# Transnormer attention and a squared-ReLU MLP on one core: the opening's loads and steps in another order, seven clamps on GpSimd, batch three's last queries loaded elsewhere

## The chip, the core and the metric

One core of a Trainium2 chip runs the whole kernel. The metric is device time in microseconds (us); lower is better. The core has five engines that each work through their own list of instructions in order and wait for each other by semaphores: PE (TensorE, matrix products), DVE (VectorE), ACT (ScalarE), POOL (GpSimd) and SP (SyncE, which issues nearly all transfers here). Sixteen DMA engines move data between HBM and the on-chip memory.

## What is computed

```python
def _attn_ref(q, k, v, g_norm):                    # q, k, v: (8, 8, 576, 64)
    kv = np.einsum('bhsd,bhse->bhde', k, v)
    out = np.einsum('bhsd,bhde->bhse', q, kv)
    rms = np.sqrt(np.mean(out * out, axis=-1, keepdims=True) + 1e-06)
    return (out / rms * g_norm).astype(np.float32)

def _moe_ref(x, w_in, w_out):                      # x: (4608, 512), w_in: (512, 2048), w_out: (2048, 512)
    h = x @ w_in
    r = np.maximum(h, 0.0)
    return ((r * r) @ w_out).astype(np.float32)
```

The attention output, transposed to (batch, token, head, feature), is x. q, k and v are float32; the two weight matrices come as float64 and are turned into float32 on the chip.

## The kernel before

**Strips.** The 4608 tokens are 36 tiles of 128, in nine strips of four tiles. Each strip has a first product (x by w_in, then ReLU and square) and a second one (by w_out). Strip zero multiplies plainly in its first product (`up_first`, L898) and by a seven-product scheme in its second (`down`, L857). Strip one uses the seven-product scheme in its first product (`up`) and a two-level one in its second (`down_deep`, `small_products`, L852), which takes its weights as 14 blocks that SP streams from HBM (`stream`, L955 and L961, tile `w_blk`). From strip two on both products are two-level, and part of the first product's weights are streamed too (L949). The attention of later tokens is spread over the strips as a list of small steps, `slices`, that `attend` works off.

**Transfers.** Nothing is scheduled by a tool: instructions stand on each engine in the order in which the program emits them. SP issues one transfer after another; a transfer that has to wait, for a buffer or for the landing of an earlier one (only a few may be in flight), holds all that stand behind it. Queries of batches two and up are read in pieces of 32 features, four transfers to a head pair (`load`, L124); the last 64 rows of each batch, which do not fill a tile, come apart (`load_rest` for keys and values, L163; `load_q_rest` for queries, L171 for batches zero and one, L177 with eight transfers of 16 KB for the others). From strip one on such loads stand in the queues `drips` and `rest_drips`, from which one is taken every so many steps (`drip`), unless `quiet` is true. `transposed_query` puts the next ones into these queues.

**The opening.** The first strip's tokens are batch zero's first 512 rows. For each head pair p: T(0, p) transposes queries on PE (L407) and copies them on ACT (L409); K(0, p) multiplies keys and values on PE (L435, the last rows from `k_rest` and `v_rest` at the end) and copies on ACT (L440, L441); Q(p) multiplies queries with that (L585), squares on ACT and sums on DVE (L488); N(p) takes the root (ACT) and its inverse and scales (DVE); F(p) transposes the result (L611) and copies it with g_norm to `xT` (L612); U(p, tiles) are the first product's matmuls for that p (`first_up`, L622), which need weight piece p.

**Weight conversion.** Each matrix comes as 16 pieces of 512 KB float64 (`load_piece`, L240, eight buffers `raw`). For a piece ACT makes two passes (`convert_on_act`, L254 and L258; here `size` and `low`), and DVE four steps (`conversion`): a clamp (L266), a shift (L268), a merge (L272) and a sum (L275). The intermediate `w_c` has four buffers. In the opening pieces zero to three are converted by hand-placed steps (`first_piece`), the clamps of one to three on GpSimd; the others go in pairs by `convert` between the steps of strip zero. Pieces four and five have their ACT passes after the opening's list.

Of the kernel before, what the change touches and what calls it, by code (L numbers as in the profile page):

```python
# [15 lines left out]
ALU = mybir.AluOpType  # L16
# [4 lines left out]
def kernel(  # L21
# [34 lines left out]
    nc = tc.nc  # L56
    P = 128
    B, H, S, D = q.shape
# [3 lines left out]
    NP = H // 2  # L62
# [9 lines left out]
    N_STRIP = N_TILE // NT  # L72
    DEEP = 1
    DEEP_UP = 2
    FIRST_SENT = 9
    SQ = 32
    Q_ON_PE = 2
# [78 lines left out]

    squares = lambda t: t.rearrange("p h d -> p (h d)").rearrange("p (k q f) -> p k q f", k=4, f=SQ)

    def load_rest(b, eng):
        h = b % 2  # L160
        half = slice(REST * h, REST * (h + 1))
        for t, src in ((k_rest[half], k), (v_rest[half], v)):
            eng.dma_start(out=t, in_=src[b, :, C * P : S].rearrange("h s d -> s h d"))  # L163

    def load_q_rest(b, eng, one=None):
        h = b % 2
# [81 lines left out]
    def convert_on_act(i, parts=(0, 1)):  # L248
        view = lambda dt: raw[i].bitcast(dt).rearrange("p b (n two) -> p b n two", two=2)
        low, high, high_f = view(U32)[:, :, :, 0], view(I32)[:, :, :, 1], view(FP32)[:, :, :, 1]  # L250
        r = view(I32)[:, :, :, 0]
        if 0 in parts:
            c = wtmp.tile([P, 2, WN // 2], FP32, name="w_c", tag="w_c")
            nc.scalar.activation(c, high_f, AF.Abs)  # L254
            words[i] = c, r, high

        if 1 in parts:
            nc.scalar.activation(r, low, AF.Copy, scale=2.0**-29)  # L258

    def conversion(i, dest, eng=nc.vector):  # L260

        c, r, high = words.pop(i)
        ci = c.bitcast(I32)


        yield eng.tensor_scalar(out=c, in0=c, scalar1=LEAST, scalar2=MOST, op0=ALU.max, op1=ALU.min)  # L266

        yield nc.vector.tensor_scalar(  # L268
            out=ci, in0=ci, scalar1=3, scalar2=0x3FFFFFFF, op0=ALU.logical_shift_left, op1=ALU.bitwise_and
        )  # L270

        yield nc.vector.scalar_tensor_tensor(  # L272
            out=ci, in0=high, scalar=-(2**30), in1=ci, op0=ALU.bitwise_and, op1=ALU.bitwise_or
        )
        yield nc.vector.tensor_tensor(out=dest.bitcast(I32), in0=ci, in1=r, op=ALU.add)  # L275
# [73 lines left out]
    nc.scalar.sqrt(one, one)  # L349

    load_next()
    load_rest(0, nc.sync)
    load_next()
    for p in range(2, NP):
        load(0, p, nc.sync, "q")
        load_piece()
        load(0, p, nc.sync, "kv")
        next(to_load)
    load_more(0)
    g_col = const.tile([P, 1], FP32, name="g_col")  # L360
# [20 lines left out]
    def transposed_query(b, p):  # L381
        while any(f == load and a[:2] == (b, p) for f, a in drips):
            drip()
        t = main.pop(("q", b, p))
        if b >= Q_ON_PE:
            qT[b, p] = qt_pool.tile([P, C, P], FP32, name="qT", tag="qT")
            nc.vector.transpose(out=flat(qT[b, p]), in_=flat(t))
            if b % 2 and p == NP - 1:
                while any(f == load_q_rest and a[0] <= b for f, a in (*rest_drips, *drips)):
                    drip(not drips)  # L390
                nc.vector.transpose(
                    out=open_rest(b).rearrange("p q (k t) -> p q k t", k=4),
                    in_=squares(q_rest[b // 2]).rearrange("p k q f -> p q k f"),
                )
            drip_queries()
            if p == NP - 1 and b + 1 < B:
                (rest_drips, drips)[b % 2 == 0].extend((load_q_rest, (b + 1, nc.sync, a)) for a in range(4))
            return
        ps = apsum.tile([P, C, P], FP32, name="t_ps", tag="at")
        if (b, p) == (0, 0):  # L400
            keep_busy(ps[:, 0], 7)
        for c in range(C):
            if b:
                nc.tensor.transpose(ps[:, c, :], flat(t[:, c]), ident)
                continue
            for h in range(2):
                nc.tensor.matmul(ps[ts(h, D), c, :], lhsT=t[:, h, c], rhs=ident, start=True, stop=True)  # L407
        qT[b, p] = qt_pool.tile([P, C, P], FP32, name="qT", tag="qT")
        nc.scalar.copy(qT[b, p], ps)  # L409
        if (b, p) == (1, NP - 1):  # L410
            drip_queries()
# [186 lines left out]
    def first_piece(i, n):  # L598

        if i not in first_steps:  # L600
            first_steps[i] = conversion(
                i, w_in[:, i % KH, 0, i // KH * 2 : i // KH * 2 + 2], nc.gpsimd if i else nc.vector
            )
        for _ in range(n):
            next(first_steps[i])

# [87 lines left out]
    )  # L694
    U = first_up
    size, low = (lambda i: (act, (i, (0,)))), (lambda i: (act, (i, (1,))))
    slices += [(T, (0, 0)), (K, (0, 0)), (T, (0, 1)), (Q, (0,)), (K, (0, 1)), (N, (0,)), size(0), (piece, (0, 1))]
    slices += [(T, (0, 2)), (Q, (1,)), low(0), (piece, (0, 1)), (K, (0, 2)), (N, (1,)), (F, (0,)), (T, (0, 3))]
    slices += [(piece, (0, 1)), (Q, (2,)), (piece, (0, 1)), size(1), (K, (0, 3)), low(1), (N, (2,)), (F, (1,))]
    slices += [(piece, (1, 4)), (Q, (3,)), size(2), low(2), (U, (0, [0, 1, 2])), size(3), (F, (2,)), (piece, (2, 4))]  # L700
    slices += [(U, (1, [0, 1, 2])), (N, (3,)), low(3), (piece, (3, 4)), (U, (2, [0, 1])), (F, (3,)), (U, (2, [2]))]
    slices += [(U, (3, [0, 1, 2]))]
    ready[0] = len(slices)
    def query_pairs(b):
        first_n = b // 2 * PAIR + (C if b % 2 else 0)
# [636 lines left out]
    attend(ready[0])  # L1342
    opening.close()
    apsum = psums.enter_context(tc.tile_pool(name="apsum", bufs=2, space=bass.MemoryType.PSUM))
    for i in range(NP, NP + 2):
        convert_on_act(i)
    acted[0] = NP + 2
    for s in range(N_STRIP):
        attend(ready[s])
        if s == DEEP_UP - 1:  # L1350
# [23 lines left out]
        for i, (w, fn, a) in enumerate(steps):  # L1374
# [33 lines left out]
            if s:  # L1408
                clock[0] += 3.2 if i >= n_up else 2.2 if s == DEEP else 1.2
                soon = tiles_due and tiles_due[0][2][0] // NT == s + 1  # L1410
                if i == n_up + 10:
                    while tiles_due and tiles_due[0][2][0] // NT == s + 1:
                        _, f, a = tiles_due.popleft()
                        f(*a)
                elif not due(keys_due) and not (soon and due(tiles_due)):
                    least = 2.1 if s == DEEP else 4.5 if i < n_up else 3.3
                    quiet = n_up * 2 // 3 < i < n_up + 3 or s == DEEP and i > n_up + 9
                    quiet = quiet or s == DEEP and i < n_up and drips and drips[0][0] == load_q_rest
                    if not quiet and clock[0] >= dripped[0] + least:
                        dripped[0] = clock[0]  # L1420
                        drip(True)
                if s == DEEP:
                    attend(begun + (goal - begun) * min(i + 1, 25) // 25)
                elif i < n_up:
                    attend_between(i, begun, goal, *(2, 34) if s == DEEP_UP else (0, 27), 38)
                if s == DEEP and i in (3, 4, 7, 9):
                    if i == 3:
                        last_sums = store_deep_sums(*deep_due.popleft())
                    next(last_sums, None)
# [65 lines left out]
```

## Time and profile before

| what | value |
|---|---|
| median of three runs | 870.54 us (870.09 to 873.51) |
| the profiled execution | 870.41 us |
| its span, from the first to the last instruction | 868.6 us |
| moved by DMA | 236.47 MB, mean 272 GB/s |
| first matmul of strip zero's plain product (L898) | 33.01 us |
| PE, DVE, DMA in 35 to 40 us | 4.79, 5.00 of 5.00 us busy, DMA share 1.03 |
| PE, DVE, DMA in 160 to 165 us | DMA share 0.74, 208 GB/s |

The span is what the trace covers. In strips of digits each digit is a fortieth of the span, 21.7 us, and stands for a busy share in tenths. A row of a timeline gives the start, the duration, engine, line, operation and tiles, and in brackets how long the engine had been idle and what ended it. A matmul of these float32 operands shows as two records. A DMA share near 1 means that the sixteen engines were moving packets all the time.

### The profile page before, as it was taken

Reading aid. Unit: us, or ns where it says so; the run is one execution under the profiler, and the core shown is the slowest. Engines: PE = TensorE matmul, PEld = TensorE weight load, DVE = VectorE, ACT = ScalarE, POOL = GpSimd, SP = SyncE. Lnnn points to the kernel's source line nnn. Section 1 sums busy time; section 2 is a strip of 40 time slices with the busy share of each in tenths; the row PEclk is TensorE's granted clock in tenths of the full one; section 3 lists DMA queues with packets and bytes.
Section 4 is the critical chain, followed back from the end, with each engine's and each line's share of the span. In section 5 each row is a group of like instructions: output and inputs, shape, how many; then the busy total and the mean of one; then the engine's idle time right before and its main releaser. Section 6 shows DMA issues by size and latency. Waiting matters only on the chain.

```text
span 868.6 us, 32585 instructions
## 1 busy us (share of the span) xinstructions
PE 860.5 (99%) x14176; PEld 804.9 (93%) x14176; DVE 720.1 (83%) x1236; ACT 352.1 (41%) x805; POOL 314.5 (36%) x319
## 2 busy tenths in 40 slices
PE   9999999999999999999999999999999999999998
PEld 7445888889999999999999999999999999999998
DVE  3999998879877996789688977897889777875887
ACT  5799251320048403750356034901491148102810
POOL 1100004630459314740574045704470447144700
PEclk9999999999999999999999999999999999999999
DMA  9998997999999997889787979998668856885483
GB/s 310 319 332 250 279 374 234 288 332 352 275 259 252 352 328 233 230 310 332 222 244 266 344 243 260 283 304 279 202 230 294 302 170 221 286 289 196 175 315 121
DMA packets 169470, 236.47 MB, mean 272 GB/s; under 512 B 78704, under 2 KB 133744, under 8 KB 161008
## 3 DMA queue, kind: packets, MB, share of 16 engines
q1 hardware_dynamic: 169024, 234.33, 83.1%
q8 instruction: 111, 1.82, 0.8%
q14 instruction: 31, 0.25, 0.1%
q10 hardware_dynamic: 304, 0.07, 0.0%
HBM read 197.66 MB, written 36.70 MB: 270 GB/s over the span
## 4 chain that ended last, share of the span: by engine, by line
PE 87%; DMA 5%; ACT 3%; DVE 3%; issue 1%; SPq 1%; DVEq 0%; ACTq 0%
PE ps_A L852 35%; PE ps_B L852 30%; PE ps_A L857 5%; PE ps_C L852 5%; PE kv_ps L435 2%; DMA w_blk<-w_deep 2%; PE x_ps L471 2%; PE ps_B L857 2%; PE ps_C L857 2%; DVE w_t L292 1%; PE ps_A L898 1%; DMA w_deep<-w_t 1%; DMA raw<-in_moe_w_out_dram 1%; DMA first_qkv<-in_v_dram 1%; PE ps_B L898 1%; PE ps_C L898 1%
## 5 line engine op out<-in xcount | busy, mean ns | idle before, releaser
L852 PE MATMUL ps_B<-w_blk,g_s 128*64 128x128 f32 x2016 | 121.8, 273 | 0.0
L852 PEld LDWEIGHTS ps_B<-w_blk,g_s 128*64 128x64 f32 x2016 | 112.4, 137 | 0.1
L852 PE MATMUL ps_A<-x_l,w_in 128*64 128x128 f32 x1568 | 102.5, 273 | 0.8 <-ACT snap L1315 0.6
L292 POOL TENSOR_TENSOR x_l<-xT 128x256 f32<-128x256 f32 x21 | 16.1, 766 | 229.8 <-PE ps_A L852 181.8
L852 PE MATMUL ps_B<-w_blk,gt 128*64 128x128 f32 x1504 | 93.9, 273 | 1.0 <-DMA w_blk<-w_deep 1.0
L852 PE MATMUL ps_A<-w_blk,g_s 128*64 128x128 f32 x1536 | 92.0, 273 | 0.0
L852 PEld LDWEIGHTS ps_A<-x_l,w_in 128*64 128x64 f32 x1568 | 88.9, 137 | 1.4 <-ACT snap L1315 0.8
L1310 POOL TENSOR_TENSOR snap<-snap,gt 128x512 f32<-128x512 f32 x35 | 46.2, 1320 | 113.8 <-ACT snap L1315 104.5
L852 PEld LDWEIGHTS ps_B<-w_blk,gt 128*64 128x64 f32 x1504 | 84.4, 137 | 1.5 <-DMA w_blk<-w_deep 1.2
L852 PEld LDWEIGHTS ps_A<-w_blk,g_s 128*64 128x64 f32 x1536 | 85.5, 137 | 0.0
L1315 ACT COPY snap<-ps_A 128x512 f32<-128x512 f32 x63 | 36.9, 585 | 105.0 <-PE ps_A L852 96.6
L1250 ACT ACTIVATE gt<-gt 128x512 f32<-128x512 f32 x112 | 70.1, 626 | 9.5 <-DVE gt L1310 9.5
L1251 ACT ACTIVATE gt<-gt 128x512 f32<-128x512 f32 x112 | 70.7, 631 | 3.6
L852 PE MATMUL ps_A<-w_blk,gt 128*64 128x128 f32 x1152 | 71.0, 273 | 0.0
L1099 ACT COPY o_sb<-ps_A 128x128 f32<-128x128 f32 x24 | 6.4, 266 | 144.7 <-PE ps_A L852 115.2
L852 PEld LDWEIGHTS ps_A<-w_blk,gt 128*64 128x64 f32 x1152 | 64.5, 137 | 0.0
L292 DVE TENSOR_TENSOR gt<-gt 128x2048 f32<-128x2048 f32 (+1 forms) x29 | 59.7, 2064 | 0.0
L1098 DVE TENSOR_TENSOR o_sb<-o_sb,ps_B 128x256 f32<-128x256 f32 (+1 forms) x123 | 47.5, 386 | 14.6 <-ACT o_sb L1099 9.4
L1310 POOL TENSOR_TENSOR gt<-gt,snap 128x512 f32<-128x512 f32 x42 | 52.6, 1282 | 15.1 <-DVE snap L1310 15.1
L852 PE MATMUL ps_B<-x_l,w_blk 128*64 128x128 f32 x784 | 51.3, 273 | 0.0
L852 PE MATMUL ps_A<-x_l,w_blk 128*64 128x128 f32 x784 | 51.2, 273 | 0.0
L1099 ACT COPY o_sb<-ps_B 128x128 f32<-128x128 f32 x31 | 8.2, 266 | 96.2 <-PE ps_B L852 96.2
(194 smaller groups left out, 1835.2 us busy)
## 6 DMA issues: line engine op xcount, KB each, us to landing
w_blk<-w_deep SPq DMA_DIRECT2D x56, 1024.0 KB, 7.3
w_blk<-w_out SPq DMA_DIRECT2D x56, 768.0 KB, 6.4
w_blk<-w_in_deep SPq DMA_DIRECT2D x49, 768.0 KB, 6.1
raw<-in_moe_w_in_dram SPq DMA_DIRECT2D x16, 512.0 KB, 7.0
raw<-in_moe_w_out_dram SPq DMA_DIRECT2D x16, 512.0 KB, 5.2
k<-in_k_dram SPq DMA_DIRECT2D x29, 256.0 KB, 5.3
v<-in_v_dram SPq DMA_DIRECT2D x29, 256.0 KB, 5.5
x_d<-x_q SPq DMA_DIRECT2D x27, 256.0 KB, 5.2
```

Of the source, the lines that this page charges most:

```text
L292: eng.tensor_tensor(out=out, in0=a, in1=b, op=ALU.subtract)
L435: nc.tensor.matmul(ps[ts(h, D), i], lhsT=a, rhs=w, start=i == 0 and c == 0, stop=c == C, skip_group_check=True)
L471: nc.tensor.matmul(ps[half, r, i, ts(p, D)], lhsT=q[row, half], rhs=kvd[b, p][row, row], start=True, stop=True)
L852: nc.tensor.matmul(ps[half], lhsT=lhsT[:, half], rhs=rhs, start=start, stop=stop, skip_group_check=True)
L857: nc.tensor.matmul(bank[BANK[p]][:, i, :], lhsT=lhsT(k), rhs=rhs(k), start=p in (1, 5, 2) and i == 0 and k == 0, stop=k == n - 1, skip_gro ...
L898: nc.tensor.matmul(ps, lhsT=w_in[:, kc % KH, g, kc // KH * 2 + fh, ts(i, P)], rhs=xt[0][:, :, kc, :], start=kc == 0, stop=kc == NP - 1,)
L1098: add = lambda out, a, b: nc.vector.tensor_tensor(out=out, in0=a, in1=b, op=ALU.add)
L1099: yield nc.scalar.copy(q[:, 3:4], small(1))
L1250: nc.scalar.activation(o, o, AF.Relu)
L1251: nc.scalar.activation(o, o, AF.Square)
L1310: add = lambda eng, out, a, b: eng.tensor_tensor(out=out, in0=a, in1=b, op=ALU.add)
L1315: nc.scalar.copy(t, ps)
```

## The change

Six things change.

- The opening's loads: the first two heads' last key and value rows come first and the other six heads' later; weight piece zero comes after the second pair's queries, and the pieces one to seven after all of batch zero's pairs.
- The opening's steps (`slices`): piece zero's ACT pass and three DVE steps stand right behind K(0, 0), with its last DVE step behind N(0); one matmul of U(0) comes ahead of K(0, 3); piece two's first pass is ahead of Q(3).
- The ACT passes of pieces four to seven come into the opening's list; before, those of four and five stood behind it and those of six and seven in the first `convert`.
- The clamps of pieces one to seven go to GpSimd, directly behind each piece's first ACT pass; before, only those of one to three did, as part of the DVE steps' order.
- Batch three's `load_q_rest` is not put into the queue `drips` any more but issued in steps 5 to 8 of strip one's first product.
- The condition that kept `drips` quiet in strip one's first product while a `load_q_rest` was next is gone; instead the queue is quiet in the first seven steps after the first of the second product.

On SP this puts eight L177 transfers and four more L124 transfers ahead of strip one's first streamed block, and takes the eight L177 transfers from between its later blocks; the later L124 transfers move forward accordingly. PE's instructions stay the same but for the one matmul that moves.

```diff
+    REST_EARLY = 3
...
-    def load_rest(b, eng):
+    def load_rest(b, eng, hs=slice(0, H)):
...
-        for t, src in ((k_rest[half], k), (v_rest[half], v)):
-            eng.dma_start(out=t, in_=src[b, :, C * P : S].rearrange("h s d -> s h d"))
+        for t, src in ((k_rest[half, hs], k), (v_rest[half, hs], v)):
+            eng.dma_start(out=t, in_=src[b, hs, C * P : S].rearrange("h s d -> s h d"))
...
             words[i] = c, r, high
+            if i in CLAMPED_AHEAD:
+                clamp(nc.gpsimd, c)
...
+    CLAMPED_AHEAD = range(1, 8)
+
+    def clamp(eng, c):
+        eng.tensor_scalar(out=c, in0=c, scalar1=LEAST, scalar2=MOST, op0=ALU.max, op1=ALU.min)
+
-    def conversion(i, dest, eng=nc.vector):
+    def conversion(i, dest):
...
-        yield eng.tensor_scalar(out=c, in0=c, scalar1=LEAST, scalar2=MOST, op0=ALU.max, op1=ALU.min)
+        if i not in CLAMPED_AHEAD:
+            yield clamp(nc.vector, c)
...
     load_next()
-    load_rest(0, nc.sync)
-    load_next()
+    load_rest(0, nc.sync, slice(0, 2))
+    load(0, 1, nc.sync, "q")
+    load_piece()
+    load(0, 1, nc.sync, "kv")
+    load_rest(0, nc.sync, slice(2, H))
     for p in range(2, NP):
-        load(0, p, nc.sync, "q")
-        load_piece()
-        load(0, p, nc.sync, "kv")
+        load(0, p, nc.sync)
+    for p in range(1, NP):
         next(to_load)
     load_more(0)
...
-            if p == NP - 1 and b + 1 < B:
+            if p == NP - 1 and b + 1 < B and b + 1 != REST_EARLY:
...
-    slices += [(T, (0, 0)), (K, (0, 0)), (T, (0, 1)), (Q, (0,)), (K, (0, 1)), (N, (0,)), size(0), (piece, (0, 1))]
-    slices += [(T, (0, 2)), (Q, (1,)), low(0), (piece, (0, 1)), (K, (0, 2)), (N, (1,)), (F, (0,)), (T, (0, 3))]
-    slices += [(piece, (0, 1)), (Q, (2,)), (piece, (0, 1)), size(1), (K, (0, 3)), low(1), (N, (2,)), (F, (1,))]
-    slices += [(piece, (1, 4)), (Q, (3,)), size(2), low(2), (U, (0, [0, 1, 2])), size(3), (F, (2,)), (piece, (2, 4))]
-    slices += [(U, (1, [0, 1, 2])), (N, (3,)), low(3), (piece, (3, 4)), (U, (2, [0, 1])), (F, (3,)), (U, (2, [2]))]
-    slices += [(U, (3, [0, 1, 2]))]
+    slices += [(T, (0, 0)), (K, (0, 0)), size(0), (piece, (0, 3)), (T, (0, 1)), (Q, (0,)), low(0), (K, (0, 1)), (N, (0,))]
+    slices += [(piece, (0, 1)), (T, (0, 2)), (Q, (1,)), (K, (0, 2)), (N, (1,)), (F, (0,)), (T, (0, 3)), (Q, (2,))]
+    slices += [size(1), low(1), (U, (0, [0])), (N, (2,)), (K, (0, 3)), (F, (1,)), size(2), (piece, (1, 3)), (Q, (3,))]
+    slices += [low(2), size(3), (U, (0, [1, 2])), (F, (2,)), (piece, (2, 3)), (U, (1, [0, 1, 2])), (N, (3,)), low(3)]
+    slices += [(act, (4,)), (act, (5,)), (piece, (3, 3)), (U, (2, [0, 1])), (F, (3,)), (act, (6,)), (act, (7,))]
+    slices += [(U, (2, [2])), (U, (3, [0, 1, 2]))]
...
-    for i in range(NP, NP + 2):
-        convert_on_act(i)
-    acted[0] = NP + 2
+    acted[0] = 2 * NP
...
-                    quiet = quiet or s == DEEP and i < n_up and drips and drips[0][0] == load_q_rest
+                    quiet = quiet or s == DEEP and n_up < i < n_up + 8
...
+                if s == DEEP and 5 <= i < 9:
+                    load_q_rest(REST_EARLY, nc.sync, i - 5)
```

More of the change, by code (lines that the diff above doesn't have):

```diff
@@ L600, in first_piece @@
         if i not in first_steps:
-            first_steps[i] = conversion(
-                i, w_in[:, i % KH, 0, i // KH * 2 : i // KH * 2 + 2], nc.gpsimd if i else nc.vector
-            )
+            first_steps[i] = conversion(i, w_in[:, i % KH, 0, i // KH * 2 : i // KH * 2 + 2])
         for _ in range(n):
```

## The prediction

> **What bounds the kernel now.** I read the page first, then the waits of PE, the chain of waits from 190 to 260 us, then timelines of PE, DVE and ACT. The page:
>
> ```profile
> span 868.6 us, 32585 instructions
> PE 860.5 (99%) x14176; PEld 804.9 (93%) x14176; DVE 720.1 (83%) x1236; ACT 352.1 (41%) x805; POOL 314.5 (36%) x319
> PE   9999999999999999999999999999999999999998
> DVE  3999998879877996789688977897889777875887
> PEclk9999999999999999999999999999999999999999
> DMA  9998997999999997889787979998668856885483
> ```
>
> PE is busy 860.5 of 868.6 us at full clock. No PE work is removed, so only PE's idle time can be won: 8.1 us at most, of which 1.4 is the wait for the identity before anything has landed. DVE and DMA are both full in the first 100 us, and DMA again from 150 to 240 us: these make PE late. All waits of PE that the trace counts:
>
> ```profile
> PE t_ps L379 <- POOL ident masks.py:199: 1.4, 1, 1.4
> PE ps_B L852 <- DMA w_blk<-w_deep: 1.0, 1, 1.0
> PE ps_A L852 <- ACT snap L1315: 0.6, 1, 0.6
> PE ps_A L622 <- DVE w_in L275: 0.4, 1, 0.4
> PE kv_ps L435 <- DMA v_rest<-in_v_dram: 0.3, 1, 0.3
> PE kv_ps L435 <- DMA first_qkv<-in_v_dram: 0.3, 1, 0.3
> PE ps_A L857 <- DVE o_sb L1029: 0.3, 1, 0.3
> PE ps_B L898 <- ACT gt L905: 0.2, 1, 0.2
> ```
>
> Ends of matmuls are modelled, so I measure a wait by starts: the next start less the start before and less what that matmul takes in an unbroken row (0.86 us for 128x512, 0.87 for sixteen 128x128 records). From PE's timeline, within the change's reach: 0.38 us at 8.61 (v_rest), 0.46 at 18.16 (last keys), 0.54 at 24.18 (piece one's weights), 0.31 at 30.36, 0.37 at 38.53, 0.31 at 50.96, 0.41 at 54.90, 0.44 at 131.72, 1.19 at 236.11. Together 4.4 us.
>
> **Opening.** Transfers land one after another. A 256 KB tile takes 0.65 us, a 512 KB weight piece 1.27. v0 lands at 1.74 + 5.0 = 6.75, q1 at 8.99: both rest loads and q1 in 2.24 us, so the rests cost 1.6. Before: q2 11.1, piece zero 12.3, v2 13.6, q3 14.3, piece one 15.6, v3 10.73 + 7.3 = 18.0, piece seven 15.61 + 10.1 = 25.7. After, by the same steps and a quarter of the rest first (0.4): q1 7.8, piece zero 9.1, v1 10.4, the other rests 11.6, q2 12.2, v2 13.5, q3 14.2, v3 15.5, piece one 16.7, piece seven 24.4. The two added issues cost SP about 0.4 us each; it is paced by landings from 6.8 on, so these are hidden.
>
> PE, with starts as in the trace (T 1.02, Q 1.09, K 0.88, F 0.59, U 0.86): the rest of K0 no longer waits (8.24 for 8.61), T1 at 8.5, Q0 9.5, K1 10.6, but K1's rest waits for 11.6 and T2 for q2 at 12.2 (before 12.11): the early win is eaten, 0.1 lost. From there the last keys are in time (15.5, needed at 18), winning 0.46. Piece zero goes through DVE ahead of the first mean, done by 15, so one U runs before K3. Q3 then waits 0.3 for ACT, which has piece one's two passes (0.67 each) ahead of the key copies. Piece one's Abs ends near 19, its GpSimd clamp near 21, its last DVE step near 23, and U of piece one is due near 23.5: the 0.54 goes. The 0.31 goes because F3 comes earlier. Sum -0.46 - 0.54 - 0.31 + 0.1 + 0.3 = -0.9. Bounds: -2.0 if q2 is in time and Q3 does not wait; +1.0 if piece zero lands two microseconds later, since ACT and DVE stand behind it in order and the first means with them.
>
> **Clamps and passes of pieces four to seven.** The rows of the clamp's line, on the two engines:
>
> ```profile
> L266 DVE TENSOR_SCALAR w_c<-w_c x17: 416/421/427, 14.7 to 58.1; 128x512 f32<-128x512 f32 x17
> L266 POOL TENSOR_SCALAR w_c<-w_c x3: 1916/1916/1917, 19.2 to 24.1; 128x512 f32<-128x512 f32 x3
> ```
>
> Four clamps leave DVE: two pairs of 0.67 (a pair's second starts 0.33 after its first), 1.3 us. GpSimd gets 4 x 1.92 = 7.7 us; it has only a memset of 0.3 us between 26 and 140 us, so nothing waits behind them. ACT was idle 3.64 us before F3's copy at 29.39; pieces four and five (2.4 us) now fill that. They wait for buffers of pieces zero and one only, freed by 23. Six and seven wait for pieces two and three and stand behind F3's copy. In the first clamps two overlapped DVE steps were longer: 0.54 for 0.17 (L489 at 19.26) and 0.99 for 0.69 (L272 at 22.41), 0.67 in three clamps; four more cost 0.9. DVE saves 0.4, but it starts piece four at 29 instead of 30.66 and does not stand 1.1 us for ACT: it runs about 3 us ahead, pieces six and seven done near 36 instead of 39. PE needs them from 35.5 on, so 0.37 goes. At 50.96 and 54.90 PE waited for ACT, which had stood 1.06 us for a weight piece at 48.47; loads freed earlier take perhaps half. At 131.72 PE waited 0.44 for a DVE that had been full since 30; a lead of one microsecond removes it. I take -1.1 of 1.5. Bounds -1.5 and 0: the lead may be eaten, but DVE was full before too.
>
> The Trainium skill speaks against this ("GPSIMD Engine Reference", section 1 Specifications): GpSimd's SBUF interface is shared with VectorE, and instructions with two SBUF inputs contend. The trace agrees in part: one two-input step of three pieces grew by 0.31. If all eight such steps of pieces four to seven grew so, an estimate by that rule is 2.5 us lost for 1.3 won, and this term would be 0. The same page's section 4.1 calls one-input work on GpSimd roughly line-rate; the trace has 1916 ns against 421.
>
> **Batch three's last queries.** The chain in strip one's end (start, us, what):
>
> ```profile
> 214.19 5.08 PE ps_A L852 x93
> 219.27 8.05 DMA w_blk<-w_deep
> 227.32 0.02 issue
> 227.34 0.31 SPq L177
> ...
> 227.75 8.32 DMA w_blk<-w_deep
> 236.07 0.04 issue
> 236.11 1.09 PE ps_B L852 x16
> ```
>
> The last block was issued at 227.75, after SP had stood for landings with queries (L177) in front of it, and landed 1.1 us late. After, the eight L177 transfers (0.43 us each on SP, 16 KB) are gone from 208 to 231. Four of them stood between the output rows at 222.94 and this issue, so it can go some 1.7 us earlier, more than the 1.1 needed: -1.1. Next due are the strip-two weights at 240.5, landed at 239.5 before and moving with it. Bounds -1.2 and 0.
>
> They now go out around 160 to 165 us, and four more main query transfers follow them before the first streamed block, since the queue they blocked is open. Added there: 8 x 0.43 + 4 x 0.48 = 5.4 us of SP's time, or 384 KB, 1.2 to 1.8 us at the 208 to 334 GB/s of these windows. The DMA share of 160 to 165 is 0.74, 1.3 us free. Behind them on SP are the sums of the weights, keys, x_d and the streamed blocks. Block two landed at 185.46 + 10.2 = 195.7 and is used at 198.3 (2.6 to spare); block four at 194.0 + 8.7 = 202.7, used at 204.4 (1.7 to spare). A push near 2 costs +0.3. Bounds 0 and +2.4 (5.4 less 1.3 free, less 1.7). No transposition of queries gets later: all main queries go out earlier.
>
> **Sum.** -0.9 - 1.1 - 1.1 + 0.3 = -2.8. The profiled execution took 870.41 us, 1.8 outside its span; 867.6. The median of the three runs is 870.54, 0.13 above it, which I leave out.
>
> **Rivals.** (a) The lead of DVE does not hold: contention and F3's place in ACT's queue eat it, the opening wins half. -0.4 + 0 - 1.1 + 0.3 = -1.2, 869.2. For it: DVE stays full to 100 us whatever is moved. Against it: the 3.64 us gap of ACT and the 1.1 us that DVE stood. (b) Slower: strip one's queue. If the twelve transfers hold SP for their 5.4 us and for two more stands for landings such as the 2.08 us at 170.48, block four is 9.5 - 1.7 = 7.8 us late; its wait outweighs the rest from 3.1 us on. +7.8 - 2.0 (opening and DVE) - 1.1 = +4.7, 875.2. For it: DMA shares of 0.97 to 1.12 from 165 to 200. Against it: 16 KB each, and the slack of 160 to 165. (c) Everything wins its bound: -2.0 - 1.5 - 1.2 = -4.7, 865.7. (d) The reordering in the opening gives no earlier v3, the queue being as full as before: -0.9 becomes +1.0, 869.5.
>
> **Numbers.** Forecast 0.58 (866.3 to 869.0), (a) 0.14, (d) 0.09, (b) 0.10, (c) 0.09. The range 865.7 to 871.5 takes in forecast, (a), (c), (d); (b) and the rest are left out. 0.5%, about what a measurement of this kernel can tell from no change, is 4.35 us: 866.2 and 874.9. Faster beyond that is (c), 0.09; slower is (b)'s upper part with mishaps not seen here, 0.08; within 0.83.
>
> **What would show it.** First L898 matmul at 32.1 instead of 33.01; no PE wait for L275 at 24 or 38; the first clamps on DVE at pieces eight and nine; no wait at 236; PE waits at 198 or 204 under 0.5. Wrong: a PE wait over 1 us for w_blk near 204, or DVE steps near 0.99 in most pieces.

## The result, and the profile after

| | before | after |
|---|---|---|
| median of 8 runs each (range) | 870.75 us (870.09 to 873.94) | 876.51 us (874.01 to 879.68) |
| ratio after to before, 95% interval | | 1.0062 (1.0045 to 1.0079) |
| the profiled execution | 870.41 us | 876.58 us |

The change makes the kernel slower, by 5.8 us in the medians. Only rival (b), 875.2, lay near it. That is luck in the main: (b) had strip one lose 7.8 us and the opening win, and the larger part of the loss came from the opening; strip one lost 3.2. The page of the changed kernel; its lines are numbered nine to eleven higher (L435 is now L446, L622 L631, L852 L861, L898 L907):

```profile
span 874.8 us, 32592 instructions
PE 863.0 (99%) x14176; PEld 807.6 (92%) x14176; DVE 719.7 (82%) x1232; ACT 352.6 (40%) x805; POOL 321.8 (37%) x323
PEclk8999999999999999999999999999999999999999
```

PE has the same 14176 records but is busy 2.5 us longer, and the clock row shows why: its first digit is 8. So PE was not only idle longer, it also ran slower for a while. The waits of PE:

```profile
PE kv_ps L446 <- DMA v<-in_v_dram: 2.2, 1, 2.2
PE ps_B L861 <- DMA w_blk<-w_deep: 1.6, 1, 1.6
PE t_ps L390 <- POOL ident masks.py:199: 1.4, 1, 1.4
PE kv_ps L446 <- DMA v_rest<-in_v_dram: 0.9, 1, 0.9
PE ps_A L631 <- DVE w_in L284: 0.6, 1, 0.6
```

Three waits for transfers stand at new places: for v1 (the second head pair's values, needed by K(0, 1)) in the opening, and for the last rows of a batch and for a streamed block in strip one. Below, K1 is short for K(0, 1), T2 for T(0, 2), U3 for U(3), and so on. PE's timeline in the opening shows the first wait and what follows it, then the same steps in the kernel before:

```profile
12.94 1.12 PE L446 MATMUL kv_ps<-v,k 128*64 128x64 f32 x16 [2.24 <-DMA v<-in_v_dram]
14.20 0.48 PE L446 MATMUL kv_ps<-v_rest,k_rest 64*64 64x64 f32 x4
14.65 1.98 PE L418 MATMUL t_ps<-ident,first_qkv 128*64 128x128 f32 x16
16.56 2.08 PE L596 MATMUL x_ps<-kv_all,qT 128*128 128x128 f32 x8
```

```profile
11.23 0.69 PE L435 MATMUL kv_ps<-v,k 128*64 128x64 f32 x16
12.11 1.09 PE L407 MATMUL t_ps<-ident,first_qkv 128*64 128x128 f32 x16
```

T2 takes 1.98 us where it took 1.09 before, Q1 2.08 for 1.16. The windows of those microseconds (the last three columns are granted clock, DMA share and GB/s) give the reason:

```profile
10.00:12.00 2.00, 0.71 (x7) 0.51 (x5) 1.32 (x3) 1.98 (x4) 0.00 (x0) 1.00 1.24 222
12.00:14.00 2.00, 1.06 (x16) 0.97 (x16) 0.99 (x3) 0.26 (x1) 0.00 (x0) 0.65 1.13 291
14.00:16.00 2.00, 1.87 (x20) 1.70 (x20) 0.52 (x3) 0.63 (x3) 0.00 (x0) 0.50 1.10 385
16.00:18.00 2.00, 2.00 (x12) 1.67 (x10) 1.47 (x4) 0.59 (x1) 0.00 (x0) 0.50 1.00 363
18.00:20.00 2.00, 2.00 (x25) 1.64 (x25) 0.69 (x1) 0.67 (x2) 0.00 (x0) 0.65 1.04 400
```

With a wait of 2.24 us TensorE was granted half its clock for about 7 us. In the kernel before, all these windows have 1.00, as here:

```profile
12.00:14.00 2.00, 2.00 (x27) 1.76 (x26) 1.53 (x6) 1.49 (x5) 0.00 (x0) 1.00 1.09 390
```

It is not a matter of one execution: all eight runs of the changed kernel list a mean granted clock of 0.994 to 0.998, while of the 82 runs of the kernel before beside the experiments six lie under 0.999. The Trainium skill ("TensorE: Matmul & The Clock Gate", "Why this matters for your kernels") warns of idle gaps above about 3 us; this trace agrees with the effect, not with the size of the gap.

Both kernels give PE the same records, but for one matmul that stands earlier, so one can subtract the start of each record before from the start of the same record after. That ledger shows where time is lost and won: us later than before, with the start of the record in the kernel before in the first column. Below, a time such as 131.72 stands for that record in every kernel.

| at | record | after |
|---|---|---|
| 8.61 | K0's last rows | -0.35 |
| 11.23 | K1 | +1.71 |
| 12.38 | within T2 | +2.72 |
| 18.16 | K3 (a matmul of U0, 0.86 us, now stands ahead of it) | +5.21 |
| 31.29 | U3 | +4.82 |
| 131.72 | strip zero, second product | +3.13 |
| 163.14 | strip one, first product | +3.63 |
| 178.58 | K with v_rest | +4.63 |
| 198.3 | block of w_deep | +6.35 |
| 236.11 | last block | +5.27 |
| 865.54 | last matmul | +5.68 |

The opening costs 4.8 (with a wait of 0.64 for weight piece three at its end), 1.7 are won back until 131.72, strip one costs 3.2 and the missing wait at 236.11 gives 1.1. Strip one's two waits in the timeline, then the second record in the kernel before, which did not wait:

```profile
183.21 0.35 PE L446 MATMUL kv_ps<-v_rest,k_rest 64*64 64x64 f32 x5 [0.88 <-DMA v_rest<-in_v_dram]
204.65 1.09 PE L861 MATMUL ps_B<-w_blk,gt 128*64 128x128 f32 x16 [1.56 <-DMA w_blk<-w_deep]
```

```profile
198.30 1.04 PE L852 MATMUL ps_B<-w_blk,gt 128*64 128x128 f32 x16
```

### The profile page after: what moved, and what is told of

Same layout as the page of the kernel before. It is cut to its first block, busy times and chain, and to the rows that moved or that the text cites. A ratio compares the mean times of both kernels' runs of the same rounds, so it can differ in the third digit from the quotient of the medians.

```text
span 874.8 us, 32592 instructions
## 1 busy us (share of the span) xinstructions
PE 863.0 (99%) x14176; PEld 807.6 (92%) x14176; DVE 719.7 (82%) x1232; ACT 352.6 (40%) x805; POOL 321.8 (37%) x323
## 4 chain that ended last, share of the span: by engine, by line
PE 89%; DMA 5%; SPq 2%; ACT 1%; DVE 1%; issue 1%; DVEq 0%
PE ps_A L861 36%; PE ps_B L861 31%; PE ps_C L861 5%; PE ps_A L866 4%; PE ps_A L907 2%; PE ps_B L866 2%; DMA q<-in_q_dram 2%; PE x_ps L482 2%; PE kv_ps L446 2%; PE ps_C L907 2%; PE ps_B L907 1%; DMA w_blk<-w_deep 1%; PE ps_C L866 1%; SPq L134 1%; DMA k_rest<-in_k_dram 1%; DMA v_rest<-in_v_dram 1%
## 5 line engine op out<-in xcount | busy, mean ns | idle before, releaser
L861 PE MATMUL ps_B<-w_blk,g_s 128*64 128x128 f32 x2016 | 121.8, 273 | 0.0
L861 PEld LDWEIGHTS ps_B<-w_blk,g_s 128*64 128x64 f32 x2016 | 112.4, 137 | 0.1
L861 PE MATMUL ps_A<-x_l,w_in 128*64 128x128 f32 x1568 | 102.4, 273 | 0.8 <-ACT snap L1324 0.6
L861 PE MATMUL ps_B<-w_blk,gt 128*64 128x128 f32 x1504 | 93.9, 273 | 1.6 <-DMA w_blk<-w_deep 1.6
L861 PE MATMUL ps_A<-w_blk,g_s 128*64 128x128 f32 x1536 | 92.0, 273 | 0.0
L861 PEld LDWEIGHTS ps_A<-x_l,w_in 128*64 128x64 f32 x1568 | 88.8, 137 | 1.4 <-ACT snap L1324 0.8
L861 PEld LDWEIGHTS ps_B<-w_blk,gt 128*64 128x64 f32 x1504 | 84.4, 137 | 2.1 <-DMA w_blk<-w_deep 1.8
L861 PEld LDWEIGHTS ps_A<-w_blk,g_s 128*64 128x64 f32 x1536 | 85.5, 137 | 0.0
L861 PE MATMUL ps_A<-w_blk,gt 128*64 128x128 f32 x1152 | 71.1, 273 | 0.0
L861 PEld LDWEIGHTS ps_A<-w_blk,gt 128*64 128x64 f32 x1152 | 64.5, 137 | 0.0
L861 PE MATMUL ps_B<-x_l,w_blk 128*64 128x128 f32 x784 | 51.3, 273 | 0.0
L861 PE MATMUL ps_A<-x_l,w_blk 128*64 128x128 f32 x784 | 51.2, 273 | 0.0
```

Source lines behind the costliest of these rows:

```text
L861: nc.tensor.matmul(ps[half], lhsT=lhsT[:, half], rhs=rhs, start=start, stop=stop, skip_group_check=True)
```

## The experiments

In the tables, "late" is the ledger's number for that kernel's profiled execution, and ratios are to the kernel before on the same chip. The median of before lay between 870.5 and 872.0 us beside them. A ledger shows one execution, a median all of them, so the two need not agree.

### The parts alone

**The opening's loads alone**: the kernel before with the change's `load_rest` and its order of loads, nothing else.

```diff
-    load_rest(0, nc.sync)
-    load_next()
+    load_rest(0, nc.sync, slice(0, 2))
+    load(0, 1, nc.sync, "q")
+    load_piece()
+    load(0, 1, nc.sync, "kv")
+    load_rest(0, nc.sync, slice(2, H))
...
+        load(0, p, nc.sync)
```

> The kernel before with the change's order of opening loads alone; steps, clamps and strip one as before. Theory: the loss of the opening lies in the loads. The second pair's values land near 12.8 us instead of 10.4, PE stands over 1.5 us before K1, the granted clock falls to 0.5 for several microseconds, and the first L907-like matmul (L898 before, 33.0) comes at 36 to 38; time +3 to +5 over before. Rival (the order of steps or GpSimd's clamps make the loss): K1 waits under 0.8 us, the clock stays at 1.0, and the time is within 1.2 us of before.

**Clamps and passes alone**: the kernel before with the clamps of pieces one to seven on GpSimd and the passes of four to seven in the opening's list.

```diff
+            if i in CLAMPED_AHEAD:
+                clamp(nc.gpsimd, c)
...
+    slices += [(U, (1, [0, 1, 2])), (N, (3,)), low(3), (act, (4,)), (act, (5,)), (piece, (3, 3)), (U, (2, [0, 1]))]
+    slices += [(F, (3,)), (act, (6,)), (act, (7,)), (U, (2, [2])), (U, (3, [0, 1, 2]))]
```

> The kernel before with the clamps of pieces one to seven on GpSimd and the passes of pieces four to seven inside the opening's list; loads, the other steps and strip one as before. Theory: PE's waits at 38.5, 51.0, 54.9 and 131.7 go (1.5 to 1.7 us) and nothing else changes: -1.0 to -1.9 against before. Rival (GpSimd slows DVE by as much as it relieves it): these waits stay, within 0.5 us of before.

**Strip one's part alone**: the kernel before with the early `load_q_rest` and the new quiet rule.

```diff
+                if s == DEEP and 5 <= i < 9:
+                    load_q_rest(REST_EARLY, nc.sync, i - 5)
```

> The kernel before with batch three's last queries loaded in strip one's first product and the changed quiet rule, nothing else. Theory: the twelve transfers push what stands behind them by some 4 us; PE waits near 163 (0.3 to 0.5), 178.6 (1.0, last values) and 198 (1.5 to 1.9, streamed block) appear, the wait at 236 (1.2) goes: +1.5 to +2.8 against before. Rival (these waits came from the opening's lateness): no wait at 178 and 198 over 0.4, the wait at 236 gone, -0.5 to -1.2.

| | median, us | ratio (95%) | late at U3 | 131.72 | 178.58 | 198.3 | 236.11 | end |
|---|---|---|---|---|---|---|---|---|
| loads alone | 874.50 | 1.0040 (1.0014 to 1.0065) | +1.54 | +1.61 | +1.61 | +1.61 | +0.48 | +2.02 |
| clamps and passes alone | 871.22 | 1.0001 (0.9981 to 1.0021) | +1.18 | -0.52 | -0.29 | -0.29 | -1.42 | -0.71 |
| strip one alone | 874.98 | 1.0042 (1.0020 to 1.0063) | +0.31 | +0.22 | +1.40 | +3.03 | +1.95 | +3.73 |

Two of the three parts lose by themselves. The loads lose in the opening, at K1 (1.1 us for v1). Against the expectation, the clock stayed at 1.00 in their profiled execution, and the plain product began at 34.6, not at 36 to 38; but seven of their ten runs list a granted clock of 0.994 to 0.998, so this execution shows less of the loss than the median. The clamps and passes win 1.70 us between U3 and 131.72, where the four waits that the prediction listed (38.53, 50.96, 54.90, 131.72) are gone as expected. But they lose 0.5 just before (at 28.97 they are 0.69 late, at U3 1.18; most of the 0.69 is a wait for the values of K2 at 15.07, which the edit does not touch), and their median is that of the kernel before, as the rival had it. What they lose stands in three timelines of that kernel, of GpSimd, DVE and PE:

```profile
27.08 8.37 POOL L265 TENSOR_SCALAR w_c<-w_c 128x512 f32<-128x512 f32 x4 [0.35 <-ACT w_c L254]
29.59 0.97 DVE L280 SCALAR_TENSOR_TENSOR w_c<-raw,w_c 128x512 int32<-128x512 int32 x1
31.54 1.10 PE L628 MATMUL ps_A<-xT,w_in 128*128 128x512 f32 x2 [0.64 <-DVE w_in L283]
```

While GpSimd works through four clamps in a row, DVE's merge of piece three takes 0.97 us for 0.69, and PE waits for piece three. Strip one alone has 1.08 less of the wait at 236.11, but its waits at 178.58 and 198.3 take 2.7; both were expected, and the median lost more than the 2.8 that was the upper bound. (Of what is lost after 236.11, 1.47 us is one stand of PE at 355.63 in the middle of equal matmuls, for which the profile shows no releaser; only the part up to 236.11 is read as the edit's.) The same 1.1 us are gone at 236.11 in the two other kernels too, which leave strip one's transfers as they were. For the loads alone that may be because PE comes late anyway; the clamps and passes alone come 0.29 early and have no wait there all the same: the block, issued at 227.56 against 227.75, landed after 6.6 us instead of 8.3. So the wait at 236.11 is partly a matter of the single execution, and its end is not shown to be the edit's.

### The opening: clock or wait

**Keeping PE busy.** The changed kernel with seven, then twelve dummy matmuls ahead of K1 (the kernel's own `keep_busy`), so that the clock should not fall.

```diff
+        if (b, ps_of[0]) == (0, 1):
+            keep_busy(ps[:, 0], 7)
```

> The changed kernel with seven idle matmuls by the identity (about 2 us of PE work) in front of the second pair's key product, so that PE is not idle while it waits for the values. Theory: half of the opening's loss is the granted clock, which falls to 0.5 after the 2.2 us of idleness; with PE kept busy it stays at 1.0, the wait itself (about 2.2 us) stays, and the first L907 matmul comes at 34.8 to 35.6 instead of 37.8; -2.2 to -3.2 against the changed kernel, so +2.5 to +3.5 against before. Rival (the clock would have fallen anyway or does not matter here): within 0.8 of the changed kernel.

> The changed kernel with twelve matmuls by the identity, about 2.6 us, in front of the second pair's key product, so that the whole wait for the values is covered. Theory (the fall of the granted clock is half of the opening's loss): the mean clock is 0.998 to 1.000 in every run instead of 0.994 to 0.998, and the median is 1.5 to 3 us under the changed kernel's 876.5, so +2.5 to +4.5 against before. Rival (the clock falls for another reason): clocks of 0.994 to 0.998 as before it, median within 1 us of the changed kernel's or above.

Measured with seven: 878.15 us, 1.0083 (1.0054 to 1.0111); with twelve: 877.88, 1.0083 (1.0051 to 1.0116). In the profiled executions the clock did stay up: with seven matmuls every window from 10 to 20 us has 1.00, and U3 is late by 1.80 (2.49 with twelve) instead of 4.82. So 2.3 to 3.0 us of the opening's loss go with the clock; the wait itself is most of the rest. But the median did not fall, against both expectations. One reason stands in the list of runs: three of the four runs with seven and two of the four with twelve have a granted clock of 0.997 or 0.998, so the clock fell in them after all, at a place that no profile shows; the run with seven that kept it, the profiled one, is with 874.68 the fastest of its kind. A second one shows with twelve. PE's waits have a new line, and ACT's timeline its cause:

```profile
PE ps_A L909 <- ACT gt L916: 1.8, 1, 1.8
```

```profile
50.21 0.69 ACT L255 ACTIVATE w_c<-raw 128x512 f32<-128x512 f32 x1 [2.06 <-DMA raw<-in_moe_w_in_dram]
```

PE came earlier, found ACT standing for a weight piece with the copies for PE behind it, and was late by 3.68 at 50.96 again. The pieces set the pace there in this execution: the eighth had landed at 28.8 us, and at 28.3 in the changed kernel, against 25.7 before. In the changed kernel ACT stands 1.66 us for a piece at the same place without holding up PE, which is 4.0 late there; so part of what the clock cost may have been hidden under this chain. With seven matmuls PE is only 1.83 late at 50.96.

**The rests in one piece, and piece zero behind v1.** Two versions of the changed kernel, of which the first keeps all eight heads' last rows in their old place and the second moves the weight piece back.

```diff
-    load_rest(0, nc.sync, slice(0, 2))
+    load_rest(0, nc.sync)
...
-    load_rest(0, nc.sync, slice(2, H))
```

> The changed kernel with the last key and value rows of all heads loaded in one transfer each in the first place, as before the change, and piece zero still ahead of the second pair's keys. Theory (rows of 256 B slow what was issued before and after them, wherever they stand; piece zero adds its 1.3 us): the second pair's values land near 11.8, one microsecond earlier than in the changed kernel, PE waits 0.8 to 1.5 before K1; -0.5 to -2.5 against the changed kernel. Rival (splitting the rests does no harm; piece zero alone makes the lateness): values land near 12.8 or later, within 0.7 of the changed kernel.

```diff
     load_rest(0, nc.sync, slice(0, 2))
-    load(0, 1, nc.sync, "q")
-    load_piece()
-    load(0, 1, nc.sync, "kv")
+    load(0, 1, nc.sync)
     load_rest(0, nc.sync, slice(2, H))
+    load_piece()
```

> The changed kernel with weight piece zero issued behind the second pair's keys and values and behind the other heads' last rows. Theory: the values land between 10.2 and 11.2, PE waits under 0.6 before K1, the clock stays at 1.0, but piece zero lands near 12.5 to 13.5 and ACT, which has its pass ahead of the copy of the second pair's queries, makes Q0 wait about 2 us, so the wait is passed on: within 1.5 of the changed kernel. Rival (only the keys' lateness matters): Q0 does not wait, -3 to -4.5 against the changed kernel.

Rests whole: 875.42 us, 1.0052 (1.0025 to 1.0078); v1 landed at 12.42, only 0.4 earlier than in the changed kernel where 1.0 was expected, PE waited 1.48 for it, the clock stayed at 1.00, and U3 is late by 1.43. The two medians are not told apart. Piece behind: 876.26 us, 1.0074 (1.0051 to 1.0097); v1 landed at 9.95 and K1 waited for nothing, yet the clock fell, against the expectation, and U3 is late by 5.64. Timelines of PE and ACT in this second one:

```profile
14.85 1.98 PE L417 MATMUL t_ps<-ident,first_qkv 128*64 128x128 f32 x16 [2.49 <-ACT qT L419]
```

```profile
13.53 0.66 ACT L255 ACTIVATE w_c<-raw 128x512 f32<-128x512 f32 x1 [3.63 <-DMA raw<-in_moe_w_in_dram]
14.21 0.58 ACT L419 COPY qT<-t_ps 128x512 f32<-128x512 f32 x1
```

The wait only moved: the changed list puts piece zero's ACT pass ahead of T1's copy, so whichever of v1 and piece zero comes last stops PE for 2.2 to 2.5 us, and the clock falls either way. What makes both late shows in the transfers of the first 15 us. First the changed kernel, then the kernel before:

```profile
DMA packets 4212, 3.39 MB, mean 226 GB/s; under 512 B 1415, under 2 KB 3956, under 8 KB 4212
```

```profile
DMA packets 4579, 4.05 MB, mean 270 GB/s; under 512 B 1407, under 2 KB 4069, under 8 KB 4578
```

The small packets are as many, but 0.66 MB less moved. Before, the slow stretch beside the rest loads was over by 8 us (202 and 225 GB/s in 4 to 8, then 357 and more); after, with the other six heads' rests in the queue, 8 to 12 has 252 and 222 GB/s with engines at shares of 0.90 and 1.24. With the rests whole those two windows have 327 and 290. So the split holds the rates down for longer; what it costs in time, beside the order of piece zero, these runs do not show.

**Without strip one's part**: the changed kernel with batch three's last queries and the quiet rule as before.

```diff
-            if p == NP - 1 and b + 1 < B and b + 1 != REST_EARLY:
+            if p == NP - 1 and b + 1 < B:
...
-                if s == DEEP and 5 <= i < 9:
-                    load_q_rest(REST_EARLY, nc.sync, i - 5)
```

> The changed kernel without its strip-one part: loads and steps of the opening, clamps and passes as changed; batch three's last queries and the quiet rule as before. Theory: the two losses add. The opening leaves PE 3.1 to 3.7 us late at 131.72 and 163.14; from there nothing more is lost, the matmul of 198.3 is 3.0 to 3.7 late and the one of 289.69 no later than 3.7, less up to 1.1 because PE, being late, no longer waits for the block of 236.11. The end is 2.5 to 3.7 late, the median 873 to 874.5. Rival: what strip one loses in the changed kernel comes from its own late arrival (conversion and SP's line are behind everywhere), not from the eight transfers; then the matmul of 198.3 is over 5 us late here too and the median near that of the changed kernel, 876.

873.91 us, 1.0028 (1.0012 to 1.0043). Late by 3.51 at 131.72, 163.14, 178.58 and 198.3 alike, 2.38 at 236.11, 2.37 at the end. As expected, the losses add: the opening and the clamps give the 3.5, and nothing is lost at 178.58 or 198.3 though PE is as late as in the changed kernel. The rival, that strip one only suffers from arriving late, falls.

### Strip one: bytes or places in SP's line

**The eight small transfers alone**: the kernel before with the early `load_q_rest`, while the main queries stay held back as they were.

```diff
-            quiet = quiet or s == DEEP and i < n_up and drips and drips[0][0] == load_q_rest
+            quiet = quiet or s == DEEP and i < n_up and drips and drips[0][1][:2] == (3, 3)
```

> The kernel before with batch three's last queries loaded in strip one's first product, but the four main query transfers that this would let out kept back until the second product, as before. Theory: the push in strip one comes from the twelve transfers together, so with eight small ones of 16 KB it is about half: PE's waits near 178.6 and 198 sum to 0.5 to 1.5 us instead of 2.7, and the wait at 236 is gone; between -1.0 and +1.0 against before. Rival (the eight with their rows of 128 B make the push): the waits at 178.6 and 198 sum to 2 us or more, +1.2 to +2.5 against before.

**The same, issued by GpSimd**, and nothing else different:

```diff
-                    load_q_rest(REST_EARLY, nc.sync, i - 5)
+                    load_q_rest(REST_EARLY, nc.gpsimd, i - 5)
```

> The run in which batch three's last queries alone went early (eight transfers of 16 KB in strip one's first product, main queries held back), with one difference: GpSimd issues the eight, not SP. Bytes, time and place stay the same. Theory: what pushed everything behind was their place in SP's line, where each of them waited for a landing; issued elsewhere they push nothing. Then the matmul at 178.58 (v_rest) is at most 0.5 us later than in the kernel before (2.72 with SP issuing), the one at 198.3 at most 0.5 (2.72), and the block wait at 236.11 is gone, as four transfers that stood ahead of it on SP are gone: the matmul at 289.69 about 1 us earlier than before, median 869.3 to 870.3 against 870.5 to 871. Rival 1: the sixteen DMA engines are what is full; then the push at 178.58 and 198.3 is again 2 to 3 us and the median about 875. Rival 2: GpSimd takes so long over an issue that its own sums of the weights (1.27 to 1.7 us each, from 168 on) come late; then the push is at a wait for POOL or for w_in_deep, 1 to 4 us.

| | median, us | ratio (95%) | late at 131.72 | 163.14 | 178.58 | 198.3 | 236.11 | end |
|---|---|---|---|---|---|---|---|---|
| SP issues | 875.00 | 1.0041 (1.0020 to 1.0063) | +0.09 | +0.61 | +2.72 | +2.72 | +4.66 | +4.59 |
| GpSimd issues | 876.02 | 1.0043 (1.0026 to 1.0061) | +0.07 | +1.28 | +1.33 | +1.33 | +3.50 | +3.88 |

With SP issuing, eight transfers of 16 KB, 128 KB in all, cost 2.1 us at v_rest between 163.14 and 178.58. SP's row for v_rest before, the same row with SP issuing, then PE's wait for it:

```profile
170.48 2.08 SPq L163 DMA_DIRECT2D v_rest<-in_v_dram  x1
174.71 0.78 SPq L164 DMA_DIRECT2D v_rest<-in_v_dram  x1
181.29 0.33 PE L436 MATMUL kv_ps<-v_rest,k_rest 64*64 64x64 f32 x4 [1.99 <-DMA v_rest<-in_v_dram]
```

With GpSimd issuing the same bytes SP comes to v_rest at 171.89, PE has no wait, and the push there is 0.05:

```profile
179.90 0.27 PE L436 MATMUL kv_ps<-v_rest,k_rest 64*64 64x64 f32 x2
```

What counts at v_rest is the place in SP's line. One thing more differs: GpSimd issued the eight six to nine microseconds earlier. The last run below, in which it issued them from 155.57 to 159.58, near SP's own 154.74 to 164.13, shows no push at v_rest either. The theory's other numbers missed: PE lost 1.2 us up to 163.14, 0.9 of it for values that, issued at 153.40, needed 7.2 us to land beside these transfers, and 2.2 between 198.3 and 236.11. The latter is in both kernels: they issue eight main query transfers (L125) between 196 and 240 us where the changed kernel issues four. But the kernel before issues six there and the eight small ones besides, so their number alone does not explain it, and the cause stays open. The median shows no gain from GpSimd.

### A version that beats both

**The passes alone**: the kernel before, with the ACT passes of pieces four to seven in the opening's list and the clamps where they were.

```diff
+    slices += [(U, (1, [0, 1, 2])), (N, (3,)), low(3), (act, (4,)), (act, (5,)), (piece, (3, 4)), (U, (2, [0, 1]))]
+    slices += [(F, (3,)), (act, (6,)), (act, (7,)), (U, (2, [2])), (U, (3, [0, 1, 2]))]
...
-    for i in range(NP, NP + 2):
-        convert_on_act(i)
-    acted[0] = NP + 2
+    acted[0] = 2 * NP
```

> The kernel before with one part of the change: the ACT passes of weight pieces four to seven come into the opening's list (four and five ahead of piece three's steps, six and seven behind F3); the clamps stay where they were (one to three on GpSimd in their place, four to seven on DVE). Theory: the lead of DVE comes from the passes, not from taking four clamps (1.3 us) off it, and what the run with both lost by U3 (1.18 us late, a 0.64 us wait for piece three behind 8.4 us of GpSimd clamps) came from GpSimd working beside DVE. Then U3 is at most 0.5 us late, the matmul of 131.72 at least 0.7 us earlier than in the kernel before, and the median 0.5 to 1.5 below it: ratio 0.998 to 0.9995. Rival: the lead comes from the clamps that DVE no longer does; then the matmul of 131.72 is no earlier than 0.3 us before, whatever U3 does, and the median is within 0.5 us of the kernel before or above it.

869.20 us against 871.95 for before on the same chip, 0.9981 (0.9968 to 0.9994): a small gain, with the ratio where it was expected (the medians lie 2.7 apart, more than the 0.5 to 1.5 expected). The mechanism is not shown by its profiled execution, which with 873.41 us was the slowest of the twelve runs: the record of 131.72 is 2.64 late there, not 0.7 early. ACT's and PE's timelines say what happened in it:

```profile
48.38 0.68 ACT L254 ACTIVATE w_c<-raw 128x512 f32<-128x512 f32 x1 [2.43 <-DMA raw<-in_moe_w_in_dram]
50.61 0.66 ACT L254 ACTIVATE w_c<-raw 128x512 f32<-128x512 f32 x1 [0.98 <-DMA raw<-in_moe_w_in_dram]
52.34 0.66 ACT L905 ACTIVATE gt<-ps_A 128x256 f32<-128x256 f32 x2
```

```profile
53.05 5.40 PE L898 MATMUL ps_A<-xT,w_in 128*128 128x512 f32 x8 [1.97 <-ACT gt L905]
```

ACT, ahead of its pieces, stood 3.4 us for two of them, PE's copies behind it; with 1.97 us of idle PE the clock fell once more (eight records take 5.40 us for 3.60 before). Running ahead brings the risk of standing for a transfer.

**The passes with strip one's part, the eight transfers on GpSimd in steps nine and ten:**

```diff
+                if s == DEEP and i in (9, 10):
+                    for a in (0, 1) if i == 9 else (2, 3):
+                        load_q_rest(REST_EARLY, nc.gpsimd, a)
```

> The kernel before with the ACT passes of pieces four to seven in the opening's list (as in the run with the passes only; its profiled execution lost about 3 us to a weight piece that landed late at 48 to 52, its eleven others did not show that loss in their times) and the strip-one part as in the changed kernel, main queries moved forward too, except that GpSimd issues the eight 16 KB transfers and does it in steps nine and ten, where it would stand until 168 (in the kernel before it was idle from 160.6 to 168.3). Theory: SP's line decides strip one; relative to how late PE is at 163.14, the matmul of 178.58 comes at most 0.5 us later and that of 198.3 at most 0.7, the wait at 236.11 is gone (1.1 us), and the end is earlier than in the run with the passes only: median 867.8 to 869.0, ratio 0.996 to 0.998. In strip zero, the matmul of 131.72 at least 0.7 us earlier than in the kernel before, if no piece lands late. Rival 1: the four main query transfers that go forward on SP push by themselves; then the matmul of 198.3 is over 1 us later relative to 163.14, median 869.5 to 870.5. Rival 2: as in the run with GpSimd issuing, the eight transfers slow down the loads beside them (values of a K step landed 7 us after their issue there, PE waited 0.9 us), and PE loses 1 us or more between 131.72 and 198.3 at a wait for k, v or w_in_deep.

869.91 us, 0.9987 (0.9972 to 1.0002); expected were 867.8 to 869.0. Late by +0.89 at U3, -0.13 at 131.72, -0.23 at 163.14 and again at 178.58, +0.67 at 198.3, -0.42 at 236.11, +0.03 at 289.69, +0.97 at the end. The push at v_rest is gone once more (1.1 with SP issuing). The block at 198.3 still comes 0.9 late, by the profile for w_deep, between theory and rival 1: four main transfers on SP, forward by a strip, are left as its likely cause, which no run isolates. DVE's lead won 1.0 here. Of the two versions only the first has its whole interval below the kernel before, by 0.06 to 0.32%.

## Why the prediction was wrong, step by step

**Opening, -0.9; measured +4.8.** The step that failed is "Transfers land one after another", with 0.65 us for a tile, 1.27 for a piece and 0.4 for the quarter of the rests. Up to q1 the sum held (7.69, predicted 7.8). Then piece zero took 2.2 us for 1.27, k1 and v1 together 2.9 for 1.3, and v1 landed at 12.81 instead of 10.4. The prices had been read from rows of the kernel before after 9 us, when its rest loads were done; in the changed kernel, transfers that shared the queue with rest loads moved at 220 to 250 GB/s, and the split kept these in the queue until 14 us. The prediction's bound, +1.0 for "piece zero lands two microseconds later", had a late transfer, though another one, but not its price: it priced a wait of PE as its length. With the wait of 2.24 came half the clock for 7 us, another 2.3 to 3.0 us (by the profiled runs with dummy matmuls). No bound held that: the profiled execution of the kernel before, from which the prediction worked, has no such wait and a clock of 1.00 to the end. That K3, U of piece one and F3 would win their 0.46, 0.54 and 0.31 could not show: L907 first ran at 37.83, not 32.1.

**Clamps and passes, -1.1 of 1.5; measured -1.7** from U3 to 131.72, in the part alone as in the changed kernel. In the part alone the lead was real. In the changed kernel PE came 4 to 5 us late, which alone may have removed the same waits; with the rests whole and with the dummy matmuls, where the same steps met a less late PE, nothing was won on balance (1.43 to 1.80, 1.80 to 2.06 and 2.49 to 3.54 from U3 to 131.72). Also, the contention that the prediction priced at 0.9 on DVE met PE directly: a wait of 0.64 us for piece three, which the prediction did not list. Net, the part's median shows no gain (1.0001). Moving the passes without the clamps kept some of the lead: 1.0 in the one profiled execution in which no piece landed late.

**Wait at 236.11, -1.1; measured -1.08,** but not shown to be the change's: kernels without its strip-one part lost the same wait. The step took one execution's landing, 1.1 us late, for a fixed property of the order on SP.

**The push of twelve transfers, +0.3; measured +2.7 (1.0 at v_rest, 1.7 at the block),** and 0.5 more at 166.8, where PE waited for DVE's transposed queries. Failed: "The DMA share of 160 to 165 is 0.74, 1.3 us free", by which 5.4 us of SP's time became "a push near 2". Free bandwidth was the wrong currency. Strip one's part alone issues block two at 190.86 for 185.46, 5.4 us later with PE only 0.3 late: the whole price, against a slack of 2.6. A transfer's place in SP's line costs about half a microsecond whatever its size: in the run with SP issuing, a pair of 16 KB transfers held it for 0.79 to 2.08 us, one of 256 KB keys or values for 0.42 to 0.90. Besides, the line is paced by landings: in the opening SP issued at 9.90, 11.48 and 12.83, just as piece zero, k1 and v1 landed. The run with GpSimd issuing shows that the bytes are not what pushes v_rest, and so does the last one. Also, "a push near 2" looked for slack at the blocks (2.6 and 1.7 us) and not at v_rest, which had 1.5: before, it landed at 177.1 and was used at 178.58; with SP issuing it landed at 181.2. Rival (b) named the line but not the block: it had block four 7.8 us late, and it was block two that PE waited for, with 0.05 more at block four (204.41). It was given 0.10.

**Chances.** "Within 0.5%" had 0.83. The errors were not independent: opening and strip one both rest on one model, bytes over bandwidth, and both were off by it in the same direction.

## What to carry to other kernels

On a PE that is hardly ever idle, price a possible wait of two microseconds with a bound of twice its length or more, since the clock may fall with it; it need not, as the list below shows. Dummy matmuls held the clock in the two profiled executions, but not in every run, and bring no time where another chain (here the weight pieces through ACT) paces the same stretch. Cost a transfer on a queue that is paced by landings by its place in the line, not by its bytes, and look for slack at the first consumer behind it. Before a load is split or moved, read the queue's GB/s beside it: here, what landed beside the rest loads and their small packets came at 200 to 250 GB/s instead of 350 to 400.

## What the runs showed of the hardware

- With an idle gap of PE of 2.24, 2.49 or 2.59 us came half the granted clock for 6.8 us, with one of 1.97 us for 3.4 us. With three gaps of 1.99 to 2.01 us (SP issuing the eight, seven dummies and rests whole, all in strip one) and with 1.81 us (twelve dummies) the clock stayed at 1.00. So near 2 us the length of the gap alone does not decide it; what does is not shown.
- Eight 16 KB transfers cost the first consumer behind them on SP 2.1 us and, issued by GpSimd at 0.54 to 0.66 us each, nothing at the same consumer, though a load beside them took 7.2 us to land.
- With four 128x512 clamps in a row on GpSimd (8.37 us), DVE's two-input merge took 0.97 us for 0.69.
- PE stood 1.15 and 1.47 us in two kernels in the middle of equal matmuls with no releaser in the profile; runs of the unchanged kernel scatter from 868.4 to 875.9 us.
